# Cross-covariance attention and a multiplicative FFN on one core: scores folded into w1 and w2 per batch, norms by squares and sums, casting loads, and an order written by hand

## The chip, the core and the metric

The kernel runs on one NeuronCore of a Trainium2 chip. The metric is device microseconds for one execution, lower is better. A core has a matrix engine (PE, TensorE), a vector engine (DVE, VectorE), an engine for activation functions (ACT, ScalarE), a general one (POOL, GpSimd) and one that issues transfers (SP, SyncE). Each engine takes its instructions in the order in which they are written to it, and an instruction that waits holds all that stand behind it on the same engine. Data lies in HBM, in SBUF (128 partitions) and in PSUM (eight banks of 512 float32 numbers per partition, where matrix products are summed). A weight load (PEld in the profile) brings the stationary operand into PE; the other operand streams past, one column after another.

## The reference

There are B = 4 batches of N = 5824 tokens with C = 256 channels, and an FFN with F = 1024 inner channels. All inputs are float32.

```python
def _attn_ref(q, k, v, tau) -> np.ndarray:
    qn = q / (np.linalg.norm(q, axis=1, keepdims=True) + 1e-06)
    kn = k / (np.linalg.norm(k, axis=1, keepdims=True) + 1e-06)
    s = kn.transpose(0, 2, 1) @ qn / tau
    s = s - s.max(-1, keepdims=True)
    a = np.exp(s)
    a /= a.sum(-1, keepdims=True) + 1e-09
    return (v @ a).astype(np.float32)
...
def _moe_ref(x, w1, w2, w3, w_out) -> np.ndarray:
    a = x @ w1
    b = x @ w2
    h = a * b @ w3
    return (h @ w_out).astype(np.float32)
```

The attention is over channels, so the matrix `a` of a batch is only 256 x 256, and its norms run over all tokens of the batch. The output of the attention, `x = v @ a`, is the input of the FFN.

## The kernel before, in words

**Preparation (lines 55 to 91).** w1 and w2 are loaded as bfloat16 by casting transfers from POOL (L58, L59). w3 is cast into a scratch tensor in HBM (L70), read back transposed by eight DMA transposes (L74), and multiplied by w_out (L85), which gives one matrix W = w3 @ w_out of 1024 x 256 in bfloat16 (L91).

**Scores of a batch (lines 105 to 157).** The tokens are taken in pieces of eight tiles of 128 tokens; six pieces make 46 tiles, the last one half empty and filled with zeros (L114, L115). SP loads q, k and v as float32 (L117 to L128), each token's row of 1 KB on its own. ACT casts v and q to bfloat16 (L129, L130), DVE casts k (L131). SP transposes the bfloat16 v (L133) into `vT`, of which there is one buffer. For each tile and each half of the channels PE makes three products: the scores G (L140, 256 columns), q times q (L146, 128 columns) and k times k (L152, 128 columns). Only the diagonals of the last two are used.

**Norms and softmax of a batch (lines 159 to 194).** DVE multiplies the products by an identity matrix and sums (L163, L164, L167, L168), ACT takes roots (L165, L169), DVE inverts; a row of q norms is made with PE (L174) and spread over the partitions by POOL (L178). DVE scales the scores (L182), finds the largest (L186), ACT takes the exponential (L191), DVE divides by the sum into `a_bf` (L194).

**FFN of a batch (lines 196 to 260).** The padded tokens are taken in chunks of 512 columns, eleven and a half per batch. For each chunk PE first makes the attention's output xT, two halves of two products each (L209), which ACT copies to bfloat16 (L215). Then for each of eight blocks jt of 128 inner channels PE makes aT from w1 (L223) and bT from w2 (L229), two products of 512 columns each; ACT copies aT to `a_sb` (L236), DVE multiplies it by bT into `ab` (L238); PE multiplies `ab` by W into the output's sums (L244), four products of 256 columns. aT and bT share three PSUM banks (tag "ab"). After the eighth block ACT copies the output (L258) and SP stores it, 128 tokens at a time (L260).

**What sets the order.** A scheduler orders the instructions of each engine by priorities and puts in the waits; the loops above only tell it what depends on what. It places later batches' loads, casts and score products between FFN instructions where it finds room.

## Time and profile before

| | |
|---|---|
| runs of the kernel | 797.06, 803.74 and 807.34 us; median 803.74 us |
| span of the profiled execution | 798.2 us |
| busy in that span | PE 675.7, PEld 393.9, DVE 307.5, ACT 417.0, POOL 9.9 us |
| moved by DMA | 114.00 MB; read from HBM 78.91 MB, written 25.95 MB |
| first xT product (L209) | 118.1 us after the span's start |

The profiled execution's own time is its span, from the first to the last instruction; it lies inside the spread of the three runs and 5.5 us under their median. A busy time is the sum of what the profiler drew for an engine. For PE it says less than it seems to: matrix products are pipelined, each is drawn from its start until its result is out, so two that follow one another overlap in the drawing. How dense PE really is shows in the distance from one start to the next. "Idle before" is the time in which an engine did nothing just before an instruction, with what ended it. PEclk is the share of its full clock that PE was granted. In the DMA views, q1 is the queue of transfers issued by SP, and q0 that of transfers issued by POOL, which alone can cast; a "packet" there is one run of bytes on one of sixteen DMA engines. Bytes are those written, so a cast from float32 to bfloat16 reads twice what is shown.

### The profile page before, as it was taken

How to read it: one execution, taken by the hardware profiler on the slowest of the kernel's cores; microseconds unless marked ns; L12 is line 12 of the kernel's file. 1: busy time of each engine (PE TensorE's matmuls, PEld its weight loads, DVE VectorE, ACT ScalarE, POOL GpSimd, SP SyncE). 2: the span in 40 equal slices, each digit the busy share in tenths (PEclk: the TensorE clock that was granted, in tenths of full speed). 3: DMA queues.
4: the chain of work that ended last, by engine and by line, in shares of the span. 5: the costliest groups of instructions: out<-in, count | busy, mean ns of one | idle time of the engine just before them, and what ended most of it. 6: DMA issues, size and time to landing. Idle time of an engine off the chain costs nothing.

```text
span 798.2 us, 11457 instructions
## 1 busy us (share of the span) xinstructions
PE 675.7 (85%) x4314; PEld 393.9 (49%) x4376; DVE 307.5 (39%) x508; ACT 417.0 (52%) x761; POOL 9.9 (1%) x22
## 2 busy tenths in 40 slices
PE   3255259999998869999998869999999959999997
PEld 2134245555554565555554555555555725555554
DVE  0000044544443353444443353444444244444443
ACT  3032267755556655554556656555555345554553
POOL 2000000000000000000000000000000000000000
PEclk9578769999999989999999889999999969999999
DMA  9999999995109897411109980010119100110111
GB/s 278 215 247 298 266 329 338 290 292 189 53 27 202 274 333 230 137 64 36 53 28 216 296 260 21 33 53 27 54 38 193 39 0 27 54 54 27 53 47 44
DMA packets 155511, 114.00 MB, mean 143 GB/s; under 512 B 60672, under 2 KB 154880, under 8 KB 155392
## 3 DMA queue, kind: packets, MB, share of 16 engines
q1 hardware_dynamic: 153792, 109.60, 48.0%
q0 software_dynamic: 1664, 3.67, 2.5%
q8 instruction: 34, 0.56, 0.3%
q14 instruction: 21, 0.17, 0.1%
HBM read 78.91 MB, written 25.95 MB: 131 GB/s over the span
## 4 chain that ended last, share of the span: by engine, by line
PE 64%; DMA 13%; ACT 10%; SPq 5%; issue 5%; DVE 3%; ACTq 0%; POOLq 0%; DVEq 0%
PE out_ps L244 20%; PE bT L229 16%; PE aT L223 16%; DMA qk_f<-in_q_dram 5%; PE xT L209 5%; ACT o_sb L258 4%; SPq L133 3%; DMA v_f<-in_v_dram 3%; ACT qk_bf L130 2%; PE G_ps L140 2%; ACT a_sb L236 2%; DMA vT<-v_bf 2%; PE qk_ps L146 2%; PE qk_ps L152 2%; DMA qk_f<-in_k_dram 1%
## 5 line engine op out<-in xcount | busy, mean ns | idle before, releaser
L238 DVE TENSOR_TENSOR ab<-a_sb,bT 128x512 bf16<-128x512 bf16 (+1 forms) x384 | 255.3, 665 | 342.2 <-PE aT L223 155.3
L236 ACT CAST a_sb<-aT 128x512 bf16<-128x512 f32 (+1 forms) x384 | 215.3, 582 | 213.7 <-PE aT L223 179.3
L229 PE MATMUL bT<-xT_bf,w_sbuf 128*128 128x512 bf16 (+1 forms) x737 | 246.9, 372 | 16.1 <-ACT a_sb L236 14.0
L223 PE MATMUL aT<-xT_bf,w_sbuf 128*128 128x512 bf16 (+1 forms) x737 | 245.9, 372 | 2.0 <-ACT a_sb L236 0.3
L244 PE MATMUL out_ps<-W_sbuf,ab 128*128 128x256 bf16 x1472 | 226.7, 275 | 4.0 <-DVE ab L238 0.7
L244 PEld LDWEIGHTS <-ab 128*128 128x128 bf16 x1472 | 123.1, 98 | 124.7 <-DVE ab L238 89.5
L140 PE MATMUL G_ps<-qk_bf 128*128 128x256 bf16 x368 | 88.3, 294 | 36.3 <-DVE qk_bf L131 25.5
L146 PE MATMUL qk_ps<-qk_bf 128*128 128x128 bf16 x368 | 83.3, 244 | 30.9 <-ACT qk_bf L130 29.4
L229 PEld LDWEIGHTS <-w_sbuf 128*128 128x128 bf16 x768 | 75.3, 98 | 66.1 <-issue 20.8
L223 PEld LDWEIGHTS <-w_sbuf 128*128 128x128 bf16 x768 | 75.5, 98 | 62.0 <-issue 7.4
L152 PE MATMUL qk_ps<-qk_bf 128*128 128x128 bf16 x368 | 83.5, 244 | 0.1
L129 ACT CAST v_bf<-v_f 128x2048 bf16<-128x2048 f32 (+1 forms) x24 | 43.9, 1830 | 62.0 <-DMA v_f<-in_v_dram 56.4
L209 PE MATMUL xT<-vT,a_bf 128*128 128x512 bf16 (+1 forms) x192 | 67.1, 377 | 6.3 <-DVE r_inv L184 3.9
L131 DVE CAST qk_bf<-qk_f 128x2048 bf16<-128x2048 f32 (+1 forms) x24 | 28.3, 1179 | 108.3 <-DMA qk_f<-in_k_dram 98.7
L215 ACT CAST xT_bf<-xT 128x512 bf16<-128x512 f32 (+1 forms) x96 | 55.2, 575 | 19.1 <-PE xT L209 17.8
L258 ACT COPY o_sb<-out_ps 128x256 f32<-128x256 f32 (+1 forms) x184 | 55.5, 391 | 13.8 <-PE out_ps L244 13.5
L130 ACT CAST qk_bf<-qk_f 128x2048 bf16<-128x2048 f32 (+1 forms) x24 | 43.9, 1831 | 31.3 <-DMA qk_f<-in_q_dram 22.4
L140 PEld LDWEIGHTS <-qk_bf 128*128 128x128 bf16 x368 | 38.6, 105 | 43.6 <-DVE qk_bf L131 37.0
L146 PEld LDWEIGHTS <-qk_bf 128*128 128x128 bf16 x368 | 41.0, 112 | 35.3 <-ACT qk_bf L130 30.1
L152 PEld LDWEIGHTS <-qk_bf 128*128 128x128 bf16 x368 | 40.9, 111 | 12.0 <-issue 2.6
L209 PEld LDWEIGHTS <-a_bf 128*128 128x128 bf16 x192 | 18.7, 98 | 30.2 <-issue 4.4
L174 PE MATMUL qn_row_ps<-identity_f,qn_col 128*1 128x128 f32 x8 | 2.3, 395 | 20.7 <-DVE tmp L167 20.7
(37 smaller groups left out, 79.5 us busy)
## 6 DMA issues: line engine op xcount, KB each, us to landing
out_dram<-o_sb SPq DMA_DIRECT2D x180, 128.0 KB, 1.8
qk_f<-in_q_dram SPq DMA_DIRECT2D x20, 1024.0 KB, 7.8
qk_f<-in_k_dram SPq DMA_DIRECT2D x20, 1024.0 KB, 10.4
v_f<-in_v_dram SPq DMA_DIRECT2D x20, 1024.0 KB, 8.5
qk_f<-in_q_dram SPq DMA_DIRECT2D x4, 640.0 KB, 8.5
qk_f<-in_k_dram SPq DMA_DIRECT2D x4, 640.0 KB, 9.1
v_f<-in_v_dram SPq DMA_DIRECT2D x4, 640.0 KB, 8.5
scratch_w_bf<-in_moe_w_dram POOLq DMA_DIRECT2D x1, 2048.0 KB, 17.6
```

The lines of the kernel that those rows point to most:

```text
L130: nc.scalar.copy(qk_bf[:, :nt, :C], qk_f[:, :nt, :C])
L140: nc.tensor.matmul(G_ps[:, ct, :], lhsT=qk_bf[:, i, C + ct * P:C + (ct + 1) * P], rhs=qk_bf[:, i, :C], start=first, stop=last,)
L146: nc.tensor.matmul(qq_ps[:, ct, :], lhsT=qk_bf[:, i, ct * P:(ct + 1) * P], rhs=qk_bf[:, i, ct * P:(ct + 1) * P], start=first, stop=False,)
L152: nc.tensor.matmul(kk_ps[:, ct, :], lhsT=qk_bf[:, i, C + ct * P:C + (ct + 1) * P], rhs=qk_bf[:, i, C + ct * P:C + (ct + 1) * P], start=Fal ...
L209: nc.tensor.matmul(xT_ps[:, :ncur], lhsT=a_bf[:, c1t, c2t * P:(c2t + 1) * P], rhs=vT[:, n0 // P:(n0 + ncur) // P, c1t, :], start=(c1t == 0 ...
L215: nc.scalar.copy(xT_bf[:, c2t, :ncur], xT_ps[:, :ncur])
L223: nc.tensor.matmul(aT_ps[:, :ncur], lhsT=w1_sbuf[:, ct, jt * P:(jt + 1) * P], rhs=xT_bf[:, ct, :ncur], start=(ct == 0), stop=(ct == CT - 1),)
L229: nc.tensor.matmul(bT_ps[:, :ncur], lhsT=w2_sbuf[:, ct, jt * P:(jt + 1) * P], rhs=xT_bf[:, ct, :ncur], start=(ct == 0), stop=(ct == CT - 1),)
L236: nc.scalar.copy(a_sb[:, :ncur], aT_ps[:, :ncur])
L238: nc.vector.tensor_mul(ab[:, :ncur], a_sb[:, :ncur], bT_ps[:, :ncur])
L244: nc.tensor.matmul(out_ps[:, ns, :], lhsT=ab[:, ns * P:(ns + 1) * P], rhs=W_sbuf[:, jt, :], start=(jt == 0 and z_start), stop=(jt == FT - ...
L258: nc.scalar.copy(o_sb[:nvalid, ns, :], out_ps[:nvalid, ns, :])
```

## The change

The program is written anew; what it computes for each output is the same up to rounding, with the softmax's subtraction of the maximum left out.

- **Token order.** Of each batch, the first 45 x 128 tokens are loaded as `(p i) c -> p i c`: partition p holds tokens 45p to 45p+44, so that a piece of eight tiles is 8 KB in one run per partition. The 64 tokens that are left form a short last tile. The output is stored in the same order, four rows or 4 KB per partition (L318).
- **Loads.** q, k, v, w1, w2, w3 and w_out are all loaded by POOL with a cast to bfloat16 on the way (L101, L102, L339, L340, L352, L353). The casts on ACT and DVE are gone. SP has only transposes and stores.
- **Norms.** The products q times q and k times k are gone. ACT squares q and k, two tiles at a time (L146), DVE adds the squares up in float32 (L158, L171), PE sums over partitions with a column of ones (L179), and ACT makes the root with Ln and Exp (L184, L185). The k norms are spread along a row by PE (L195).
- **Scores folded into the weights.** The product is now q times k (L149), so that after the exponential `e` can be the stationary operand. Instead of xT = a^T vT for each chunk, the kernel makes a @ w1 and a @ w2 once for each batch (`Wf`: L232 on PE, then L238 on ACT and L240 on DVE, which also divide by the sums), and the FFN takes vT itself as its streaming operand (L282). The stage xT and its copies are gone.
- **FFN.** Chunks are 512 columns, eleven per batch, and a twelfth of 192. aT and bT share four PSUM banks, the output has three of 512 numbers. ACT and DVE copy one half of the output each (L316, L317), and one store of 512 KB per chunk takes it away.
- **Order.** The scheduler is off (`manual_schedule`); each engine's order is that of the calls. A table of calls with due times (`make_agenda`) is run down between FFN blocks as a counter of estimated PE time goes on. The output products follow their block two blocks later (LAG). In the first batch they are put off until W is made (L370), at 31 units of the counter and later, and up to 46 blocks of `ab` wait in SBUF. Batch 0's scores run ahead of all FFN work.

Two buffers of `vT` let the next batch's v be transposed while this one's is used.

```diff
+    ctx.enter_context(tc.manual_schedule())
+
+    nc.scalar.preload_act_table_set("natural_log_exp_and_others")
...
+    def load_piece(nm, n, pi):
+        pool = v_pool if nm == "v" else qk_pool
+        t = pool.tile([P, PIECE, C], BF16, tag=nm, name=f"{nm}_{n}_{pi}")
+        main, left = qk_main[nm, n]
+        g = LAST if pi == NP_ - 1 else PIECE
...
+        nc.gpsimd.dma_start(out=t[:, :g, :], in_=main[:, pi * PIECE : pi * PIECE + g, :])
+        pieces[nm, n, pi] = t
...
+                nc.scalar.activation(out=dst[:, :, part, :], in_=src[:, o : o + 2, :], func=AF.Square)
+                i = o + part
+                for ct in range(CT):
+                    nc.tensor.matmul(
+                        G[:, ct, :],
+                        lhsT=qt[:, i, ct * P : (ct + 1) * P],
+                        rhs=kt[:, i, :],
...
+            elif pr > 0:
+                nc.vector.tensor_add(accs[n], accs[n], sqs[0])
...
+        def fold(i):
+            h, rest = divmod(i, 4)
+            w, c1 = divmod(rest, 2)
+            m = psum.tile([P, 512], F32, tag="ab", name=f"fold_{n}_{i}", bufs=4)
+            for c2 in range(CT):
+                nc.tensor.matmul(
+                    m, lhsT=st["e"][:, c2, c1 * P : (c1 + 1) * P], rhs=w12[:, c2, w, h * 512 : (h + 1) * 512],
+                    start=(c2 == 0), stop=(c2 == CT - 1),
+                )
+            dst = Wf[n][:, c1, w, h * 512 : (h + 1) * 512]
+            if i % 2 == 0:
+                nc.scalar.activation(out=dst, in_=m, func=AF.Copy, scale=st["rs"][:, c1 : c1 + 1])
+            else:
+                nc.vector.tensor_scalar_mul(dst, m, st["rs"][:, c1 : c1 + 1])
...
+    def emit_ab(b, c, j):
+        n = chunk_cols(c)
+        tiles = []
+        for w in range(2):
+            t = psum.tile([P, 512], F32, tag="ab", name=f"{'ab'[w]}_{b}_{c}_{j}", bufs=4)
+            for ct in range(CT):
+                nc.tensor.matmul(
+                    t[:, :n], lhsT=Wf[b][:, ct, w, j * P : (j + 1) * P], rhs=rhs_of(b, c, ct),
+                    start=(ct == 0), stop=(ct == CT - 1),
+                )
+            tiles.append(t)
...
+        nc.scalar.copy(a_sb[:, :n], tiles[0][:, :n])
...
+        nc.vector.tensor_mul(ab[:, :n], a_sb[:, :n], tiles[1][:, :n])
+        pend.append((b, c, j, ab))
...
+            for jt in range(FT):
+                at(31.0 + jt, 0.87, lambda jt=jt: w_unit(jt))
...
     for b in range(B):
...
-                        nc.tensor.matmul(
-                            qq_ps[:, ct, :],
...
-                        nc.tensor.matmul(
-                            kk_ps[:, ct, :],
...
-                xT_bf = work_pool.tile([P, CT, NCHUNK], DT.bfloat16, tag="xT")
...
+        make_agenda(b)
+        for c in range(NCH):
+            for j in range(FT):
+                run_due()
+                emit_ab(b, c, j)
+                npop = 0
+                while w_ready[0] and len(pend) > LAG and npop < 2:
+                    emit_out(*pend.pop(0))
+                    npop += 1
+                    run_due()
+        run_due(1e9)
```

**Where instructions now stand.** The first place is PE in the middle of the FFN. Before, in the last batch (each product has a weight load ahead of it, mostly left out here; aT_7689 and bT_7690 are the block that follows aT_7675 and bT_7676):

```order
L223 MATMUL aT_7675<-xT_bf,w_sbuf 128x512
...
L244 MATMUL out_ps<-W_sbuf,ab 128x256
...
L229 MATMUL bT_7676<-xT_bf,w_sbuf 128x512
...
L223 MATMUL aT_7689<-xT_bf,w_sbuf 128x512
...
L244 MATMUL out_ps<-W_sbuf,ab 128x256
...
L229 MATMUL bT_7690<-xT_bf,w_sbuf 128x512
```

The change, in batch 1 and chunk 8 (a_8_4 and b_8_4 are block 4's two products, abs_8_1 and abs_8_2 the operands of blocks 1 and 2, o_8 the output's sums, q_5 and k_5 a piece of batch 2):

```order
L303 MATMUL o_8_1_3359<-W_sb,abs_8_1_3335 128x256
L149 LDWEIGHTS q_5_2859
L149 MATMUL G_2285<-k_5_2863,q_5_2859 128x256
...
L282 MATMUL a_8_4_3383<-vT_939,Wf_1913 128x512
...
L282 MATMUL b_8_4_3386<-vT_939,Wf_1913 128x512
L303 LDWEIGHTS abs_8_2_3356
L303 MATMUL o_8_0_3358<-W_sb,abs_8_2_3356 128x256
```

Before, a block's aT stood ahead of the output products and its bT behind them, and the next block's aT followed at once. Now a block's four products stand together, then the output products of the block two earlier, and score products of the next batch come between.

The second place is the start of the program. Before, SP's queue of loads began so:

```order
L117 DMA qk_f<-in_q_dram 128x8x256
L118 DMA qk_f<-in_k_dram 128x8x256
L119 DMA v_f<-in_v_dram 128x8x256
L117 DMA qk_f<-in_q_dram 128x8x256
L118 DMA qk_f<-in_k_dram 128x8x256
L133 DMA_TRANSPOSE vT<-v_bf 128x16x128
L119 DMA v_f<-in_v_dram 128x8x256
```

Of POOL's queue in the change, these are some of the rows up to its sixteenth load, in their order (row by row q_0 to q_5 and k_0 to k_5 are the pieces of batch 0, w and w_bf are w1 with w2, and w3):

```order
L102 DMA k_1_93<-in_k_dram 128x2048
masks.py:197 MEMSET ident 128x128
masks.py:199 ISA
masks.py:199 AFFINE_SELECT ident<-ident 128x128
L102 DMA q_2_99<-in_q_dram 128x2048
...
L102 DMA v_0_175<-in_v_dram 128x2048
...
L102 DMA k_5_213<-in_k_dram 128x1280
L339 DMA w_83<-in_moe_w_dram 128x2x1024
...
L102 DMA v_1_219<-in_v_dram 128x2048
L102 DMA v_2_221<-in_v_dram 128x2048
L352 DMA w_bf<-in_moe_w_dram 128x8x1024
L353 DMA wout_sb<-in_moe_w_out_dram 128x8x256
```

Loads of q, k and v came from SP in turn, with a transpose between them; now all come from POOL, q and k of the whole batch ahead of most of v and of the weights, and an instruction that makes an identity matrix stands among them.

The third place is SP in the change, with the transposes of batch 0's v, of w3 and of batch 1's v, and the first stores:

```order
L116 DMA_TRANSPOSE vT_311<-v_0_175 128x16x128
L116 DMA_TRANSPOSE vT_311<-v_1_219 128x16x128
L116 DMA_TRANSPOSE vT_311<-v_2_221 128x16x128
L359 DMA_TRANSPOSE w3T_315<-w_bf 128x32x128
L359 DMA_TRANSPOSE w3T_316<-w_bf 128x32x128
L116 DMA_TRANSPOSE vT_311<-v_3_385 128x16x128
...
L116 DMA_TRANSPOSE vT_939<-v_0_865 128x16x128
L318 DMA out_dram<-osb_0_994 128x1024
L318 DMA out_dram<-osb_1_1094 128x1024
L116 DMA_TRANSPOSE vT_939<-v_1_1017 128x16x128
```

w3's two transposes stand behind three pieces of v, and each later transpose stands ahead of stores that queue behind it.

473 lines of the change are left out of this document (288 added, 185 removed).

## The prediction, on record before the result

> **What bounds the kernel now.** I read the page's busy times first, then the chain that ended last, then a table by stretches.
>
> ```profile
> span 798.2 us, 11457 instructions
> PE 675.7 (85%) x4314; PEld 393.9 (49%) x4376; DVE 307.5 (39%) x508; ACT 417.0 (52%) x761; POOL 9.9 (1%) x22
> PE 64%; DMA 13%; ACT 10%; SPq 5%; issue 5%; DVE 3%; ACTq 0%; POOLq 0%; DVEq 0%
> 0.00:118.00 118.00, 46.67 (x376) 37.97 (x377) 13.50 (x29) 34.76 (x32) 5.74 (x13) 0.75 1.06 271
> 300.00:420.00 120.00, 118.73 (x692) 63.96 (x704) 52.19 (x75) 66.68 (x137) 0.00 (x0) 1.00 0.29 90
> 640.00:650.00 10.00, 2.72 (x6) 0.68 (x8) 4.67 (x19) 3.66 (x8) 0.55 (x1) 0.51 0.00 0
> ```
>
> The last three rows are stretches: length, then busy time of PE, PEld, DVE, ACT and POOL, then the granted clock, the DMA share and GB/s. For 118 us the DMA engines are full and PE is mostly idle; then PE is the bound, but for a hole at 640. How dense is PE in its own stage? The timeline tells, by starts:
>
> ```profile
> 739.81 1.21 ACT L258 COPY o_sb<-out_ps 128x256 f32<-128x256 f32 x4
> 740.00 0.38 PE L223 MATMUL aT<-xT_bf,w_sbuf 128*128 128x512 bf16 x1
> 740.21 0.38 PE L229 MATMUL bT<-xT_bf,w_sbuf 128*128 128x512 bf16 x1
> 740.43 0.59 PE L223 MATMUL aT<-xT_bf,w_sbuf 128*128 128x512 bf16 x2
> 752.29 1.21 ACT L258 COPY o_sb<-out_ps 128x256 f32<-128x256 f32 x4
> 280.28 0.22 PE L146 MATMUL qk_ps<-qk_bf 128*128 128x128 bf16 x1
> 280.33 0.22 PE L152 MATMUL qk_ps<-qk_bf 128*128 128x128 bf16 x1
> 280.39 0.27 PE L140 MATMUL G_ps<-qk_bf 128*128 128x256 bf16 x1
> 280.50 0.22 PE L146 MATMUL qk_ps<-qk_bf 128*128 128x128 bf16 x1
> ```
>
> A product of 512 columns holds PE for 0.215 us, one of 256 for 0.109, one of 128 for 0.055. A chunk has 36 of the first (4 of them xT) and 32 of the second, 11.25 us, but the output copies of two chunks are 12.48 us apart: PE loses 1.23 us per chunk to its neighbours.
>
> **What goes, on PE.** xT, 4 x 0.215 = 0.86 us per chunk in 46 chunks (11.5 per batch), 40 us. The products q times q and k times k, 184 x 0.055 = 10 us per batch. The padding: 11.5 chunks become 11 and a short one.
>
> **What PE then has to do once the FFN has begun.** A chunk is 32 x 0.215 + 32 x 0.109 = 10.38 us; 44 of them make 456.7. A short chunk (192 columns, 0.083 us each by interpolation) is 32 x 0.083 + 16 x 0.109 = 4.4; four make 17.6. W: 64 x 0.109 = 7.0. Scores of three batches: 3 x 92 x 0.109 = 30.1. Folds of three batches: 3 x 16 x 0.215 = 10.3. Small products: about 3. Sum **525 us**, at the granted clock of 1.00 that the dense stretch shows.
>
> **Does PE stay the bound?** The groups with shapes kept apart:
>
> ```profile
> L238 DVE TENSOR_TENSOR ab<-a_sb,bT 128x512 bf16<-128x512 bf16 x352 | 242.0, 688 | 323.5 <-PE aT L223 155.3 <-ACT a_sb L236 136.1 <-PE bT L229 24.9
> L236 ACT CAST a_sb<-aT 128x512 bf16<-128x512 f32 x352 | 203.7, 600 | 202.3 <-PE aT L223 169.8 <-remote 16.9 <-DVE ab L238 9.2
> L130 ACT CAST qk_bf<-qk_f 128x2048 bf16<-128x2048 f32 x20 | 38.0, 1902 | 21.9 <-DMA qk_f<-in_q_dram 12.9 <-PE qk_ps L152 4.7 <-PE G_ps L140 4.1
> L130 ACT CAST qk_bf<-qk_f 128x1536 bf16<-128x1536 f32 x4 | 5.9, 1474 | 9.5 <-DMA qk_f<-in_q_dram 9.5
> L182 DVE TENSOR_TENSOR s_f<-G_ps,qn_row 128x256 f32<-128x256 f32 x8 | 3.3, 415 | 2.9 <-POOL qn_row L178 2.9
> L163 DVE TENSOR_TENSOR tmp<-qk_ps,identity_f 128x128 f32<-128x128 f32 x8 | 2.3, 292 | 17.3 <-PE qk_ps L152 17.2
> ```
>
> The trace has no square of 512 columns; the casts give 0.84 ns per column and 0.19 us, so 0.62 us, between ACT's own copy of 0.60 and half the cast of 1.90. It has no float32 sum of 1024 columns; L182 and L163 give 0.96 ns per column, so 1.15 us, with 0.69 (as the product of 512) and 2.3 (twice) as bounds. ACT then has per batch 88 x 0.60 + 46 x 0.62 + 15 us (short chunk, output copies, folds, softmax, priced as L236) = 96 us, and DVE 88 x 0.69 + 22 x 1.15 + 16 = 102, at the upper bound 127. PE has 131 in such a batch (4.4 and 11 x 10.38 for the FFN, 10.0 and 3.4 for scores and folds), so both stay under it. Block by block: a block holds PE for 4 x 0.215 + 4 x 0.109 = 1.30 us, its product is ready about 2 us after its start (aT 0.64, copy 0.60, product 0.69), and its bank is wanted two blocks later, at 2.6 + 0.43 us. A square or a sum ahead of it fits into that. Before W is there, blocks come every 0.86 us and the spare is 0.2 us. So I cost the queues at 10 us in all, with 0 and 54 (44 chunks x 1.23) as the ends; if this cover failed, the banks of bT would be late first.
>
> **The start.** A cast transfer's price stands in the DMA view of two windows, 19 to 36 us and 24 to 30 us; the transposes' in 596 to 613 us:
>
> ```profile
> q0 software_dynamic: 1068, 2.92, 90.1%
> q1 hardware_dynamic: 1064, 0.68, 21.8%
> q0 software_dynamic: 48, 1.57, 121.5%
> q1 hardware_dynamic: 48, 0.05, 3.0%
> q1 hardware_dynamic: 10656, 3.07, 98.1%
> vT<-v_bf SPq DMA_TRANSPOSE x6, 4.6
> 1.27 1.02 POOL L58 DMA_DIRECT2D w_sbuf<-in_moe_w_dram  x1 [0.33 <-issue]
> 13.22 0.57 POOL masks.py:199 TENSOR_SCALAR_AFFINE_SELECT identity_f<-identity_f 128x128 f32<-128x128 f32 x1 [10.93 <-issue]
> 17.34 17.61 SPq L133 DMA_TRANSPOSE vT<-v_bf  x1
> ```
>
> 2.92 MB in 0.901 x 17 us is 191 GB/s written. A piece of 0.52 MB takes 2.75 us, q and k of a batch (5.96 MB) 31, v half of that. POOL's instruction at 13.22 stood idle for 10.93 us first. Now it stands behind four loads (11 us of transfers, issued from 1.3 us on in up to 1.02 us each, as the row of L58 shows) and ahead of the rest, which are issued at about 4.5 + 10.9 + 1 = 16.5 us, while the first four end near 13.5: a hole of 4 us, between 0 and 5. So v's first piece lands at 2.5 + 30 + 4 + 1 = 38 us, and k's last at 43.
>
> The Trainium skill, in GPSIMD Engine Reference, Instruction dispatch, gives about 6 us for the first call into freshly loaded code. The row shows 10.93 us, and by the page's 6 the hole would be gone and the sum 4 us less.
>
> From k's last piece to the FFN stands a chain. In the trace it is these two rows, 10 us from one to the other:
>
> ```profile
> 637.74 0.30 DVE tmp L163
> 647.80 0.62 PE xT L209
> ```
>
> The new chain has no products with an identity and no maximum, but three squares, the sums, Ln, Exp, two more products on PE and four folds: I take 15, between 10 and 18. So by the chain the FFN begins at 58.
>
> **A queue that the transposes now meet.** In both windows q0 and q1 moved as many packets, 1068 and 1064, 48 and 48: an engine takes one from each queue in turn, whatever their size, and the transpose begun at 17.34 held SP for 17.61 us. Six transposes and four stores (128 runs each) are 10656 packets, so a piece of v is about 1690, or 106 per engine. Behind v's first piece stand, per engine, 24 runs of q and k, 32 of w1 and w2, 16 of v, 64 of w3. One for one, the transpose ends when 3.8 MB (the first 106 of these, in part of w3) are through: 20 us, and 2.4 of its own. So 38 + 23 = **61 us** for the FFN's begin, 58 if they don't meet, 75 if the next transposes are late too. By the same count v's second and third pieces are through at about 75 and 86, and w3's two transposes, among the next loads of q and k, near 108 and 113, while PE wants W at 61 + 31 = 92. That would be 15 us of waiting, or none if they don't meet; I take 8.
>
> The Trainium skill says in DMA: Bandwidth & Descriptors, Queues, rings and completion order, that an engine changes rows only at the end of a packet of typically 9 to 17 descriptors. The rows show turns of one by one. By the page a transpose would need a dozen turns, and the sum would be that of the second rival.
>
> **In the later batches** the same queues carry 8.9 MB of loads (47 us), six transposes (14) and 6 MB of stores (22 at the first stretch's 271 GB/s), in 131 us; q and k buffers come free one by one as scores are made, so loads come in small groups and a transpose meets 16 runs, 5 us. A chunk has two output buffers, 10 us of patience. I cost them at nothing; uncovered it would be a few us per batch.
>
> **The end.** The last output product starts at 793.83 before, and the span ends at 798.2: 4 us, and I keep 4.
>
> ```profile
> 793.83 0.39 PE L244 MATMUL out_ps<-W_sbuf,ab 128*128 128x256 bf16 x2 [0.45 <-DVE ab L238]
> ```
>
> **Sum:** 61 + 525 + 8 + 10 + 4 = 608 us against the profiled span of 798.2. The runs' median lies 5.5 us above that span, their lowest 1.1 below; I add 2 and forecast **610 us**.
>
> **Rivals.**
> - *The queues still cost PE what they cost now.* For it: DVE's 0.69 of 0.86 us before W, and waits of DVE on ACT and PE all along its row. Against it: four banks for three, and two blocks between product and use. 54 us in place of 10: 654.
> - *Transposes and loads don't meet as counted* (turns of many packets). FFN from 58, no wait for W: 608 - 11 + 2 = 599.
> - *Casting loads at half the rate.* Nothing in the rows says so for runs of 4 KB; w_out's runs of 512 bytes are among those that made the 191 GB/s. Start 31 us later, and 125 of 131 us in each batch: about 650.
> - *Slower than before: SP is held by its transposes.* Place: eight transposes per later batch, each ahead of stores. If each held SP as the one at 17.34 did, 17.6 us, 10 of them covered by the output buffers, that is 24 x 7.6 = 182: 790. From a hold of 19 us on (24 x 8.8 more than 608) it is over 820, slower. Against it: one for one, a batch's transposes can't wait for more runs than there are, 47 us of them.
> - *ACT or DVE becomes the bound* only beyond 131 us per batch, over the upper bound above; no time given.
>
> **Chances.** Forecast 0.70; second rival 0.10; first 0.10; third 0.07; fourth 0.03. The likeliest one's own range is 590 to 635: begin 58 to 75, wait for W 0 to 15, queues 0 to 20, not all at one end. The two slow ones reach 654; the range is **585 to 655**. Only the fourth leaves the faster side by 2%, which is about what a measurement of this kernel can tell from no change: faster 0.97, same 0.01, slower 0.02.
>
> **What would show it.** First L282 product near 61 us; the last batch's output copies 10.4 us apart; PE idle before L370 for about 8 us, ended by a DMA; L158 near 1.15 and L146 near 0.62 us; granted clock 1.00 from 65 us on. It is wrong if chunks of the last batch take over 11 us, if L146 waits for loads after the first batch, or if stores stand behind transposes while PE waits for output banks.

## The result, and the profile after

| | before | after |
|---|---|---|
| median of the runs shown with the result | 803.63 us | 616.50 us (606.25 to 619.94) |
| ratio, with its 95% interval | | 0.760 (0.752 to 0.768) |
| span of the profiled execution | 798.2 us | 612.9 us |
| first FFN product (before: first xT) | 118.1 us | 59.0 us |
| output copies, from one chunk of the last batch to the next | 12.48 us | 10.40 us |

The forecast was 610 us, with 585 to 655 as its range: the time lies inside, and so does its sign. Ratios are taken from undisturbed runs alone, so that they need not be the quotient of the medians given. The first views of the changed kernel, by page and by stretches (length, busy time of PE, PEld, DVE, ACT and POOL with counts, granted clock, DMA share, GB/s):

```profile
span 612.9 us, 9631 instructions
PE 561.3 (92%) x3564; PEld 353.0 (58%) x3568; DVE 396.9 (65%) x566; ACT 360.6 (59%) x657; POOL 51.2 (8%) x102
```

```profile
0.00:59.00 59.00, 25.90 (x123) 16.43 (x124) 32.17 (x35) 32.12 (x56) 13.68 (x29) 0.82 1.05 196
92.00:103.00 11.00, 7.57 (x52) 4.94 (x51) 4.49 (x8) 3.44 (x7) 0.00 (x0) 0.96 1.13 222
103.00:167.00 64.00, 64.00 (x459) 45.40 (x458) 44.45 (x56) 42.23 (x78) 9.66 (x19) 0.98 1.08 186
167.00:190.00 23.00, 15.10 (x92) 9.76 (x91) 9.82 (x13) 7.85 (x15) 2.41 (x5) 0.78 1.10 175
190.00:609.00 419.00, 415.71 (x2705) 262.08 (x2706) 282.75 (x423) 254.64 (x468) 19.03 (x38) 1.00 0.42 98
```

From 190 us on PE is busy for 415.7 of 419 us at full clock: the FFN of the later batches is as dense as forecast. What PE loses, it loses in three places of the first batch: the start, a wait near 100, and a hole between 167 and 190 that the prediction did not have. Three timelines of the changed kernel show what ended each. First PE (in brackets the idle time and what ended it):

```profile
59.03 1.03 PE L282 MATMUL a<-vT,Wf 128*128 128x512 bf16 x2 [6.97 <-DMA vT<-v]
182.48 0.58 PE L303 MATMUL o<-W_sb,abs 128*128 128x256 bf16 x2 [7.90 <-ACT osb L316]
```

then ACT's copies of the output, one per chunk:

```profile
157.02 0.58 ACT L316 COPY osb<-o 128x512 f32<-128x512 f32 x1 [0.19 <-PE o L303]
165.06 0.58 ACT L316 COPY osb<-o 128x512 f32<-128x512 f32 x1 [0.19 <-PE o L303]
181.84 0.58 ACT L316 COPY osb<-o 128x512 f32<-128x512 f32 x1 [9.25 <-DMA out_dram<-osb]
191.42 0.58 ACT L316 COPY osb<-o 128x512 f32<-128x512 f32 x1 [0.45 <-PE o L303]
```

then SP's queue, where the duration is the time for which the instruction held SP (called its hold; x2 is two holds in a row):

```profile
30.89 1.44 SPq L116 DMA_TRANSPOSE vT<-v  x1
43.41 15.86 SPq L116 DMA_TRANSPOSE vT<-v  x1
72.75 27.57 SPq L359 DMA_TRANSPOSE w3T<-w_bf  x2
151.21 17.36 SPq L116 DMA_TRANSPOSE vT<-v  x1
168.67 1.83 SPq L318 DMA_DIRECT2D out_dram<-osb  x2
170.59 16.14 SPq L116 DMA_TRANSPOSE vT<-v  x1
```

Last, two rows of the DMA view, of the transpose issued at 151.21 and of the first store issued at 168.67; the last number is the time from issue to landing:

```profile
vT<-v SPq DMA_TRANSPOSE x1, 28.4
out_dram<-osb SPq DMA_DIRECT2D x1, 512.0 KB, 13.1
```

Read backwards: PE waited at 174 for ACT's copy, and ACT from 172.6 on for a buffer whose store landed at 181.8. That store held the copy of 157.02. It stood on SP behind a transpose until 168.67, and then took 13.1 us to land, where the median store of this profile takes 3.3; the transpose ahead of it landed at 179.6, 2 us before it. So the store was late by the whole time of that transpose, 28.4 us to its landing, and not by the hold of 17.4 alone. A chunk of output came every 8.0 us then (157.02, 165.06), because the backlog of blocks is worked off at two per block. With two buffers a store then has some 15 us from the copy until its buffer is wanted again; this one took 24.

The two groups that the prediction priced without a row of their own, and the wait for W:

```profile
L158 DVE TENSOR_TENSOR acc<-acc,sq 128x1024 f32<-128x1024 f32 x88 | 107.3, 1220 | 11.7 <-ACT sq L146 9.5
L146 ACT ACTIVATE sq<-q 128x512 f32<-128x512 bf16 x88 | 55.6, 632 | 3.6 <-DVE acc L158 3.3
L369 PE MATMUL w<-wout_sb,w3T 128*128 128x256 bf16 x64 | 9.3, 305 | 3.4 <-DMA w3T<-w_bf 3.4
```

### The profile page after: what moved, and what is told of

Its sections match the earlier page's. It is cut to its first block, busy times and chain, and to the rows that moved or that the text cites. A ratio compares the mean times of both kernels' runs of the same rounds, so it can differ in the third digit from the quotient of the medians.

```text
span 612.9 us, 9631 instructions
## 1 busy us (share of the span) xinstructions
PE 561.3 (92%) x3564; PEld 353.0 (58%) x3568; DVE 396.9 (65%) x566; ACT 360.6 (59%) x657; POOL 51.2 (8%) x102
## 3 DMA queue, kind: packets, MB, share of 16 engines
q0 software_dynamic: 13952, 39.46, 36.1%
## 4 chain that ended last, share of the span: by engine, by line
PE 78%; DMA 12%; SPq 6%; DVE 1%; ACT 1%; issue 1%; POOL 0%; POOLq 0%; ACTq 0%
PE o L303 25%; PE a L282 22%; PE b L282 22%; PE G L149 5%; SPq L116 5%; DMA w3T<-w_bf 4%; DMA k<-in_k_dram 4%; DMA v<-in_v_dram 2%; DMA out_dram<-osb 2%; PE fold L232 2%; SPq L359 1%; PE w L369 1%; ACT as L288 1%; DVE abs L290 1%; PE ss L179 1%
## 5 line engine op out<-in xcount | busy, mean ns | idle before, releaser
L290 DVE TENSOR_TENSOR abs<-as,b 128x512 bf16<-128x512 bf16 (+1 forms) x384 | 252.0, 658 | 169.8 <-ACT as L288 134.4
L288 ACT CAST as<-a 128x512 bf16<-128x512 f32 (+1 forms) x384 | 215.7, 562 | 187.2 <-PE a L282 96.4
L303 PE MATMUL o<-W_sb,abs 128*128 128x256 bf16 x1472 | 222.5, 274 | 8.1 <-ACT osb L316 7.9
L282 PE MATMUL a<-vT,Wf 128*128 128x512 bf16 x704 | 211.4, 382 | 7.1 <-DMA vT<-v 7.0
L282 PEld LDWEIGHTS <-Wf 128*128 128x128 bf16 x1536 | 150.1, 99 | 111.5 <-DMA vT<-v 7.5
L282 PE MATMUL b<-vT,Wf 128*128 128x512 bf16 x704 | 211.3, 382 | 0.0
L303 PEld LDWEIGHTS <-abs 128*128 128x128 bf16 x1472 | 143.9, 98 | 91.9 <-issue 8.6
L158 DVE TENSOR_TENSOR acc<-acc,sq 128x1024 f32<-128x1024 f32 x88 | 107.3, 1220 | 11.7 <-ACT sq L146 9.5
L149 PE MATMUL G<-k,q 128*128 128x256 bf16 x368 | 69.5, 297 | 20.1 <-DMA k<-in_k_dram 20.1
L146 ACT ACTIVATE sq<-q 128x512 f32<-128x512 bf16 x88 | 55.6, 632 | 3.6 <-DVE acc L158 3.3
L149 PEld LDWEIGHTS <-q 128*128 128x128 bf16 x368 | 39.0, 106 | 28.2 <-issue 11.3
L146 ACT ACTIVATE sq<-k 128x512 f32<-128x512 bf16 x88 | 55.2, 627 | 0.0
L317 DVE COPY osb<-o 128x512 f32<-128x512 f32 x44 | 30.1, 685 | 8.3 <-DMA out_dram<-osb 7.4
L316 ACT COPY osb<-o 128x512 f32<-128x512 f32 x44 | 25.8, 586 | 13.9 <-DMA out_dram<-osb 9.2
L102 POOL DMA_DIRECT2D q<-in_q_dram x24 | 13.3, 553 | 198.0 <-ACT sq L146 162.8
L102 POOL DMA_DIRECT2D v<-in_v_dram x24 | 13.1, 551 | 62.4 <-DMA vT<-v 55.9
L232 PE MATMUL fold<-w,e 128*128 128x512 bf16 x60 | 17.5, 423 | 0.8 <-ACT as L288 0.5
L238 ACT ACTIVATE Wf<-fold,rs 128x512 bf16<-128x512 f32 x16 | 11.0, 687 | 11.7 <-PE fold L232 7.4
L240 DVE TENSOR_SCALAR Wf<-fold,rs 128x512 bf16<-128x512 f32 x16 | 11.8, 748 | 5.2 <-PE fold L232 5.1
L102 POOL DMA_DIRECT2D k<-in_k_dram x24 | 13.4, 558 | 1.6 <-DMA q<-in_q_dram 1.3
L232 PEld LDWEIGHTS <-e 128*128 128x128 bf16 x64 | 6.8, 107 | 7.4 <-issue 3.9
## 6 DMA issues: line engine op xcount, KB each, us to landing
v<-in_v_dram POOLq DMA_DIRECT2D x20, 512.0 KB, 11.6
```

What stands on the lines that cost most here:

```text
L102: nc.gpsimd.dma_start(out=t[:, :g, :], in_=main[:, pi * PIECE : pi * PIECE + g, :])
L146: nc.scalar.activation(out=dst[:, :, part, :], in_=src[:, o : o + 2, :], func=AF.Square)
L149: nc.tensor.matmul(G[:, ct, :], lhsT=qt[:, i, ct * P : (ct + 1) * P], rhs=kt[:, i, :], start=(pr == 0 and part == 0 and ct == 0), stop=(pr ...
L158: nc.vector.tensor_add(accs[n], accs[n], sqs[0])
L232: nc.tensor.matmul(m, lhsT=st["e"][:, c2, c1 * P : (c1 + 1) * P], rhs=w12[:, c2, w, h * 512 : (h + 1) * 512], start=(c2 == 0), stop=(c2 == ...
L282: nc.tensor.matmul(t[:, :n], lhsT=Wf[b][:, ct, w, j * P : (j + 1) * P], rhs=rhs_of(b, c, ct), start=(ct == 0), stop=(ct == CT - 1),)
```

## The experiments

Each kernel is the change with one edit, unless it says otherwise. Times are medians of the kernel's runs; 801 to 804 us is the kernel before beside them. The change itself spans 606 to 634 us in its ten runs, and most kernels have one profile, so a gain or loss of a few us in a median says little; what is read is each profile's waits.

**The change once more.** It had six more runs and a second profile.

> The change once more, unaltered, so that it has as many runs as the variants and a second profile. If the hold of SP by a transpose depends on which loads it happens to meet, the holds before 210 us differ from the first profile by several us each, the chunks after 210 us don't (10.4 us in the last batch, 11.5 in the others), and the runs spread over 600 to 625 us, with the difference between two profiles made wholly before 210 us. If the spread has another cause (the clock, the stores), the later batches differ too.

628.4 us, 607.8 to 633.8; ratio 0.763 (0.757 to 0.770). The profiled span was 606.0. There the output copies of the same stretch are evenly spaced:

```profile
160.38 0.58 ACT L316 COPY osb<-o 128x512 f32<-128x512 f32 x1 [0.19 <-PE o L303]
168.42 0.58 ACT L316 COPY osb<-o 128x512 f32<-128x512 f32 x1 [0.19 <-PE o L303]
176.46 0.59 ACT L316 COPY osb<-o 128x512 f32<-128x512 f32 x1 [0.50 <-PE o L303]
184.28 0.58 ACT L316 COPY osb<-o 128x512 f32<-128x512 f32 x1 [0.45 <-PE o L303]
```

The longest hold of SP between 110 and 210 us was 10.4 us instead of 17.4, there is no hole, and from 212 us on the chunks of both profiles are equal to 0.1 us. The first profile's two long chunks (16.8 and 9.6 us for 8.0 each) cost 10.4 us; the second had a longer wait for W (5.8 us for 3.4) and was 3.4 us later from there on: that leaves the 7 us between them. The transpose that landed 28.4 us after its issue in the first profile landed after 19.6 here, and the store behind it 1.2 us before the copy that took its buffer again. So the hole comes and goes from run to run with the transposes' time to landing. That the wider spread of the other runs is the same thing was not seen, since they have no profile.

**Transposes against loads, at the start.** w3 and w_out are loaded behind v's fourth piece, which waits for v's first transpose.

```diff
-    nc.gpsimd.dma_start(out=w3_bf, ...)      # ahead of the folds
-    nc.gpsimd.dma_start(out=wout_sb, ...)
             at(0.0, 0.0, lambda: load_piece("v", 0, 3))
+            at(0.0, 0.0, load_w3)
```

> The loads of w3 and w_out are issued behind the fourth piece of v, which waits until v's first piece is transposed; all else is as in the change. Theory 1 (the transposes of v's first pieces share the DMA engines run for run with the casting loads behind which they were issued): without 2.5 MB of loads beside it the first transpose is through near 46 instead of 59 us, the FFN begins when the folds are done, near 52, and w3T is done at about the same time as before or a few us earlier; the span is near 606. Theory 2 (the transpose takes its 28 us whatever the loads do, or waits for v's second piece): FFN still begins at 59, w3T later, span 613 to 620. If W comes later than the FFN's earlier start allows, half the gain goes into a longer wait before L369 (3.4 us now).

616.7 us (605.8 to 628.1), ratio 0.758 (0.753 to 0.763), span 604.4. PE's timeline:

```profile
46.53 5.27 PE L232 MATMUL fold<-w,e 128*128 128x512 bf16 x16
51.63 0.59 PE L282 MATMUL a<-vT,Wf 128*128 128x512 bf16 x2
```

The FFN follows the folds without a wait, 7.4 us earlier, as theory 1 has it: the transpose was late only for the loads beside it. But w3T was ready at 101.7, hardly earlier than before (102.5), and PE, earlier by then, waited 14.0 us for it instead of 3.4. The whole gain went into the next transfer. (The lower span is that of a profile without the late hole.)

**The wait for W.** Three pairs of loads for the second batch are moved from 16, 20 and 30 units to 34, 38 and 42.

```diff
-                at(16.0, 0.0, lambda: load_qk(1, 1))
+                at(34.0, 0.0, lambda: load_qk(1, 1))
```

> The loads of the second batch's q and k pieces 2 to 4 are due at 34, 38 and 42 units instead of 16, 20 and 30, so that they don't run beside the transposes of w3; all else is as in the change. Theory 1 (w3's transposes share the DMA engines run for run with those loads): w3T is through by about 88 us instead of 102.5, PE doesn't wait before L369 (3.4 us now, 3.5 to 5 us with the slow clock behind it), and the span up to 110 us gains 4 us. The loads meet v's transposes later, so the hole at 174 us may grow or shrink; by itself the span is about 608. Theory 2 (the transposes take their 30 us alone): w3T still ends near 102 and nothing is gained.

623.0 us (599.7 to 636.7), span 614.8. SP was free of w3's transposes at 92.5 instead of 100.3, and W's products began at 91.6 and waited for nothing: the wait is explained, though w3T was ready at 94.6, later than the 88 of theory 1. The loads then met v's transposes; PE waited 12.5 us for an output copy, and no time was gained in the median. What that copy waited for was a store issued at 117.96, ahead of the next hold (21.4 us at 120.6); it landed at 139.5, 3 us after the transpose ahead of it, which was issued at 106.85 and landed at 136.3.

**Stores on another engine.** The stores are issued by ACT.

```diff
-                nc.sync.dma_start(out=rows[:, 4 * c : 4 * c + 4, :], in_=o)
+                nc.scalar.dma_start(out=rows[:, 4 * c : 4 * c + 4, :], in_=o)
```

> The stores of whole chunks (L318) are issued by ACT instead of SP, so that no store stands behind a transpose; all else is as in the change. Theory 1 (a store waits behind a transpose that holds SP for 17 us, and while 46 blocks of backlog are worked off at two per block a chunk's output is complete every 6 us, so two output buffers cover only some 6 us): PE has no hole near 174 us, L316 waits for no store, and the span is about 10 us shorter, near 603. ACT waits for DVE's half of each output copy, under 1 us per chunk, which its spare time hides. Theory 2 (the store itself is slow because the DMA engines are full of casting loads): the wait of L316 for out_dram stays, and the span is within 3 us of 613. Theory 3 (ACT is delayed by the wait before each store, 44 times about 1 us): the hole goes but later chunks are longer than 10.4 us and the span is 613 or more.

645.2 us, span 631.8: none of the three theories. (Five runs took 614.3 to 649.6; a sixth took 1028.8 us at a granted clock of 0.66, which nothing here explains. The lowest lies inside the change's own spread, so the loss is not in every run.) ACT's timeline, then SP's:

```profile
153.86 0.59 ACT L316 COPY osb<-o 128x512 f32<-128x512 f32 x1 [2.78 <-DMA out_dram<-osb]
172.63 0.36 ACTq L318 DMA_DIRECT2D out_dram<-osb  x1
173.04 0.63 ACT L146 ACTIVATE sq<-q 128x512 f32<-128x512 bf16 x1 [18.59 <-DMA vT<-v]
```

```profile
114.49 62.09 SPq L116 DMA_TRANSPOSE vT<-v  x5
```

ACT stood 18.6 us before a store, and what ended it was a transpose. In this program's list of waits the transfers of SP and ACT take eight completion semaphores in turn, and a new transfer waits for the one that had its semaphore before. For the store at 172.63 that one was the transpose issued at 142.26, which landed only at 172.53. (SP's row merges five transposes with the waits between them; the longest single hold was 12.7 us.) The dependence had only moved to an engine that PE waits for sooner (16.5 us at L282).

**A third output buffer.** Four of 46 buffers of ab pay for it.

```diff
-            o = work.tile([P, 4, D], F32, tag="o_sb", ..., bufs=2)
+            o = work.tile([P, 4, D], F32, tag="o_sb", ..., bufs=3)
```

> Three buffers of the output copies (osb) instead of two, and 42 buffers of ab instead of 46 to make room; all else, SP's order included, is as in the change. Theory 1 (stores stand behind transposes that hold SP for 16 to 17 us, and in the backlog a chunk of output comes every 8 us): a third buffer gives 8 us more patience, so of the hole of 8 us in PE near 174 us (10 us with the low granted clock behind it) at most 2 are left and the span is 603 to 606. Theory 2 (the DMA engines themselves are behind, and any number of buffers fills up): the hole only moves to a later chunk, span 610 or more. If the first theory holds, the spread between runs shrinks too, since the hold differs from run to run.

613.6 us (605.0 to 629.5), ratio 0.757 (0.753 to 0.762), span 605.7. With holds of 14.6 and 12.1 us all chunks of the backlog are 8.0 us apart. That is no proof of the third buffer: the change's second profile has no hole with two. By the landings here (160.7 and 199.4, where the copies that would have wanted those two buffers stood at 160.5 and 196.4) it saved 0.2 and 3.1 us. The spread did not shrink, so that part of the expectation failed, and the gain in the median is within the spread.

**Short runs.** q and k of all batches in plain token order, 1 KB read and 512 bytes written per run; each score is the same sum, its tokens taken in another order.

```diff
+            order = "(p i) c -> p i c" if nm == "v" else "(i p) c -> p i c"
-                src[n, : NT * P, :].rearrange("(p i) c -> p i c", i=NT),
+                src[n, : NT * P, :].rearrange(order, i=NT),
```

> q and k alone are loaded in the plain token order, each token's row a run of 1 KB read and 512 bytes written, eight times as many runs as in the change (the scores sum over tokens, so the order is free); v and the output stay partition-contiguous. Theory 1 (queues take turns run by run, whatever the size): a transpose that meets q and k loads now waits for runs an eighth as long, so the holds of SP at 151 and 171 us shrink from 17 us to under 8, the hole in PE at 174 goes, and if the casting rate stays near 200 GB/s the span is near 603. Theory 2 (short casting runs are slower, say half the rate): k's last piece of the first batch lands near 60 instead of 33 us, the FFN begins at 80 or later and the span is 635 or more. Theory 3 (neither): within 3 us of 613.

623.7 us, 622.3 to 628.5; ratio 0.780 (0.776 to 0.784); span 621.9. Both theories hold in part. From 120 to 200 us a transpose held SP for 5.1 to 7.2 us, never 16. But loading cost more: in the DMA rows of the whole span, casting loads (q0) of the change and then of this kernel,

```profile
q0 software_dynamic: 13952, 39.46, 36.1%
```

```profile
q0 software_dynamic: 53888, 39.46, 45.7%
```

took 221 us of the sixteen engines in the change (36.1% of 612.9) and 284 here. FFN began at 62.5, w3's transposes held SP until 108, and the span is 9 us over the change's first. And a hole of 4.7 us was left near 170, where SP was not held: there two stores took 20.5 and 12.9 us to land, the first of them 1 us after the transpose issued ahead of it at 147.34, which had held SP for only 6.0 us but landed after 26.4. So the partition-contiguous order of q and k is worth having for the loads and costs something at the transposes. The runs are steady, within 6 us.

**The order of PE's products.** A block's a, then the previous block's output products, then its b.

```diff
         for w in range(2):
+            if w == 1 and mid and pend:
+                emit_out(*pend.pop(0))
```

> The order of PE's products is that of the kernel before: a block's a, then the output products of the block before it, then its b (in place of a, b, then the output products of the block two earlier); four banks as in the change. Theory 1 (the two blocks between product and use are what removed the 1.23 us per chunk): DVE's product begins when b ends and takes 0.69 us, the cover is the next a's 0.43 us, so PE waits in each block, and the last batch's chunks take 11.6 us or more (12 by 0.2 us a block); the span is 660 to 690. Theory 2 (the loss before came from the xT stage and its copies, not from the order): chunks of the last batch stay at 10.4 us and the span is 613 to 625.

773.6 us (773.4 to 774.2), ratio 0.966 (0.961 to 0.971). Theory 1 has the direction, at more than twice its size. The last batch's chunks are 15.5 us apart, 1.94 us per block. The groups say why:

```profile
L305 PE MATMUL o<-W_sb,abs 128*128 128x256 bf16 x1472 | 227.5, 275 | 117.6 <-DVE abs L292 117.4
L284 PE MATMUL b<-vT,Wf 128*128 128x512 bf16 x704 | 211.1, 382 | 0.0
```

PE waits for DVE's product ahead of every group of output products, and DVE's 0.69 us begin only when b is done. So the distance between a block and its output products is worth some 157 us. I had taken the 1.23 us per chunk of the kernel before as the price of this very order. But its order is another, as its PE shows in the last batch:

```profile
748.56 0.60 PE L244 MATMUL out_ps<-W_sbuf,ab 128*128 128x256 bf16 x4
748.99 0.38 PE L229 MATMUL bT<-xT_bf,w_sbuf 128*128 128x512 bf16 x1
749.21 0.60 PE L244 MATMUL out_ps<-W_sbuf,ab 128*128 128x256 bf16 x4
749.64 0.38 PE L223 MATMUL aT<-xT_bf,w_sbuf 128*128 128x512 bf16 x1
749.86 0.38 PE L229 MATMUL bT<-xT_bf,w_sbuf 128*128 128x512 bf16 x1
750.08 0.59 PE L223 MATMUL aT<-xT_bf,w_sbuf 128*128 128x512 bf16 x2
750.70 0.59 PE L229 MATMUL bT<-xT_bf,w_sbuf 128*128 128x512 bf16 x2
751.61 0.60 PE L244 MATMUL out_ps<-W_sbuf,ab 128*128 128x256 bf16 x4
```

It takes the output products of two blocks close together (748.56 and 749.21), then six products of the next two blocks and here two of xT (left out), and only then output products again. So this run prices half a block of distance, not the order of the kernel before; what its 1.23 us per chunk were spent on stays open.

**Three banks and one block of distance.** In place of four and two.

```diff
-LAG = 2
+LAG = 1
-            t = psum.tile([P, 512], F32, tag="ab", ..., bufs=4)   # and the five others of this tag
+            t = psum.tile([P, 512], F32, tag="ab", ..., bufs=3)
```

> Three PSUM banks for aT and bT instead of four and the output products one block behind instead of two, as the kernel before had it within half a block; all else is as in the change. Theory 1 (the fourth bank and the second block are what removed the 1.23 us per chunk that PE lost to its neighbours): with the squares and sums between, a chunk takes 11 to 11.6 us, 30 to 54 us more, 640 to 667. Theory 2 (a block's bank and product come in time anyway in a block of 1.30 us; the loss before came from the scheduler's order and the copies of xT): last batch's chunks stay at 10.4 us, scoring batches lose at most 0.3 us at each tile pair, 14 us per batch at the very most, and the span is 615 to 635.

637.1 us (621.3 to 642.9), span 641.0. The last batch's chunks stay at 10.40, those of the scoring batches go from 11.5 to about 11.8, 5 us per batch: theory 2 by its mechanism, though the span lies outside its 615 to 635. The other 15 us of the longer span arose before 231 us, with a wait of PE for an output copy of 14.0 us near 149. So the first whole block of distance is what counts; the second, with the fourth bank (the two were not tried apart), is worth some 11 us over the batches after the first (5 in each scoring batch and 1 in the last).

**The identity on POOL.** A partition_broadcast is added behind all work.

```diff
+    nc.gpsimd.partition_broadcast(spread, row1[:1, 0])
```

> One partition_broadcast on POOL, the instruction that the kernel before used at L178 and the change does without, is added behind all work, on data that nothing reads. Theory 1 (the 10.93 us that POOL stood idle ahead of the identity in the kernel before were the loading of code that this program needs for partition_broadcast): POOL stands idle for some 11 us at the identity again, q's and k's third pieces are issued near 16 us, first scores and FFN begin some 4 us later, and the span is 617 to 625. Theory 2 (the idle time had to do with the transfers issued ahead of it, or with the DMA engines being busy): no idle time at the identity, and the span is that of the change plus a few us at the end.

630.7 us (one run), span 628.9. POOL's row of the identity in the change, then in this kernel:

```profile
3.79 0.29 POOL masks.py:199 TENSOR_SCALAR_AFFINE_SELECT ident<-ident 128x128 f32<-128x128 f32 x1
```

```profile
15.46 0.28 POOL masks.py:199 TENSOR_SCALAR_AFFINE_SELECT ident<-ident 128x128 f32<-128x128 f32 x1 [11.54 <-issue]
```

An instruction at the very end brings back 11.5 us at the start, and FFN begins at 63.9, 4.9 us later. Theory 1 holds: the idle time belongs to a program that uses partition_broadcast, not to the identity. The rest of the longer span is mostly a late hole, with a hold of 22.0 us at 173.1 and 13.1 us of waiting on PE.

**Three repairs together:** w3 late, q and k late, three output buffers.

> Three edits together: loads of w3 and w_out behind v's fourth piece, the second batch's q and k pieces 2 to 4 later, three output buffers (42 of ab). If each stall has the cause that I gave it, FFN begins near 47 to 52 us, w3T is through near 88, PE waits for W at most 3 us, and no hole stands at 174: 52 + 530 of products + 6 of small losses + 4 = 592 to 597. If a stall only moves on to the next transfer, 603 or more.

607.6 us (605.5 to 618.2), ratio 0.759 (0.754 to 0.764), span 604.4. FFN begins behind the folds and the wait for W is 3.7 us, close to the 3 expected; the hole is not gone, and the span is that of the expectation's second sentence, 603 or more. PE waited 7.9 us for an output copy at 139.9. The store it needed was issued at 115.08, ahead of the hold of 23.9 us at 119.4, and took 24.8 us to land; the transpose ahead of it, issued at 103.33, took 33.7.

**The same with runs a quarter as long** for q and k of the later batches, 2 KB read and 1 KB written (again the scores' tokens are only taken in another order).

```diff
-        nc.gpsimd.dma_start(out=t[:, :g, :], in_=main[:, pi * PIECE : pi * PIECE + g, :])
+            nc.gpsimd.dma_start(
+                out=t[:, :g, :].rearrange("p (h i) c -> p h i c", i=i),
+                in_=src[n, ...].rearrange("(h p i) c -> p h i c", p=P, i=i),
+            )
```

> The three edits of the last combination (w3 and w_out behind v's fourth piece, second batch's q and k later, three output buffers), and q and k of the later batches loaded in runs of 2 KB read and 1 KB written in place of 8 and 4 KB. Theory (a hold of SP is the number of transpose packets per engine, about 106, times the time of the load run that each takes its turn with): with runs a quarter as long the holds before 210 us stay under 14 us, where the last combination had 23.9 and 28.2; three buffers cover that, no hole stands in PE between 100 and 200 us, and the span is 594 to 598. Rival (holds go by the bytes that are under way, however they are cut): a hold of over 20 us stays and with it a hole of some 8 us, 603 to 610. Second rival (shorter runs load more slowly): L146 waits for loads in the first or a later batch, 605 or more.

**598.55 us, 597.6 to 602.5; ratio 0.748 (0.745 to 0.752)**: the best of all, and its seven runs lie within 4.9 us. (The profile is that of the slowest of them.) SP's queue in the last kernel and in this one:

```profile
103.33 11.66 SPq L116 DMA_TRANSPOSE vT<-v  x1
119.38 23.89 SPq L116 DMA_TRANSPOSE vT<-v  x1
```

```profile
103.63 12.44 SPq L124 DMA_TRANSPOSE vT<-v  x1
122.31 11.63 SPq L124 DMA_TRANSPOSE vT<-v  x1
```

The second transpose, with the same pieces of load issued around it, holds SP half as long and lands after 21.2 us for 38.5. One later hold is 16.6, over the 14 expected; PE has no hole between 103 and 190. The second rival's sign, a wait of the squares for loads, is not there after the start. But W was waited for 6.1 us, and early in the second batch PE waited 3.9 us for an output copy, again behind transposes that landed late (its store landed at 218.9, the last transpose ahead of it at 213.7). In a stretch where both queues have work they moved as many packets each, now of a quarter the size (122 to 128 us of this kernel):

```profile
q0 software_dynamic: 881, 0.93, 90.1%
q1 hardware_dynamic: 880, 0.34, 32.4%
```

**Those runs alone,** without the three repairs.

> Of the last combination only the shorter load runs are kept: q and k of the later batches in runs of 2 KB read and 1 KB written; w3's place, the due times and the two output buffers are those of the change. Theory (the spread and the late holes come from turns with 4 KB runs): FFN still begins at 59 and W is still waited for (3 to 7 us), but no transpose holds SP for 17 us before 210 us, the hole in PE between 160 and 190 is under 4 us, the runs lie within 6 us of each other as those with 512-byte runs did (the change's lie 28 us apart), and the median is 604 to 610. Rival (two buffers are too few for any hold over 8 us, so short runs alone don't help): holes of 4 us and more stay in several chunks, 612 or more. Second rival (it was the three output buffers and the later loads that made the last combination steady): the runs spread over more than 15 us.

612.8 us (610.2 to 622.8), ratio 0.768 (0.762 to 0.773), span 610.2. No hold between 118 and 210 us was over 10.7 and the backlog's chunks are all 8.0 us apart, which speaks against the first rival. But the change's second profile, with long runs, has the same (10.4), so one profile does not show that the short runs did it. The wait for W rose to 11.1 us, 7.7 more than in the change's first profile, and by that the median missed its range. Five of the six runs lie within 5.4 us, the sixth 7 above them: 12.6 us in all, between the theory's 6 and the second rival's 15, so that of the steadiness it remains open how much each of the edits gives.

## Why the prediction was right, and where it was not

Time by time, the profiled span against the sum:

| term | predicted | measured |
|---|---|---|
| FFN begins | 61 | 59.0 |
| PE's products from there on | 525 | 527 (counted by groups, at the same durations) |
| wait for W | 8 | 3.4 |
| hole in the late first batch | 0 | 10 (23.0 us of stretch, 12.5 of products in it) |
| waits of PE for ACT and DVE ("the queues") | 10 | 3 |
| PE's lower clock and the rest | 0 | 6, of them 3 by a granted clock of 0.80 in the first 14 us |
| end | 4 | 4 |

The sum came out 5 us low, and that is closer than its terms: the hole and the lower clock, both put at nothing, and the products took 19 us more than forecast, and the begin, the wait for W and the queues 14 less. That much of the hit is luck.

- **The bound.** Right: PE is dense, ACT and DVE stay under it. The last batch's chunks are 10.40 us for 10.38; squares 0.63 for 0.62, sums 1.22 for 1.15. The first rival (54 us lost to the queues) falls with the 10.40. (PE's 131 us for a later batch add up to 132 by their own terms, and it took 135; nothing hangs on that.) The granted clock was 1.00 in the 419 us from 190 on, but not from 65 on as forecast: 0.78 in the stretch with the hole.
- **The start.** Right in sum, with errors that cancel, which is luck. "A hole of 4 us, between 0 and 5": there is none, and the loads ran at 214 GB/s for 191, so v's first piece landed at 30.9 instead of 38 and k's last at 34.4 instead of 43; the chain behind it took 17.7 us for 15. The step that failed is that the 10.93 us belonged to the instruction; the broadcast experiment shows what they belong to. The Trainium skill's 6 us (GPSIMD Engine Reference, Instruction dispatch) for freshly loaded code fits neither: 10.93 and 11.54 with the broadcast, nothing without it. And the transpose took 28.1 us for 23. That it met the loads is shown by moving them away (16.6 us).
- **The wait for W.** Its place and cause are right (shown by the late loads), its size smaller: w3T's halves were done at 81.5 and 102.5, not 108 and 113, and PE came to the second half only at 99.1, not at 92.
- **The step that failed** is the term at nothing: "a transpose meets 16 runs, 5 us. A chunk has two output buffers, 10 us of patience. I cost them at nothing". For the later batches, for which it was worked out, it holds: transposes held SP for 1 to 10 us and landed within 13, and PE did not wait. The late first batch had no term of its own. There the prediction's own sign of being wrong came true, stores behind transposes while PE waits for output banks: it is the fourth rival's mechanism, at one place instead of 24, 10 us in the first profile and nothing in the second. Its numbers do not fit there. The backlog brings a chunk every 8.0 us, where I had used the 10.4 of a later batch; even so two buffers give a store some 15 us, more than the 10. What was missed is that a store waits until the transpose ahead of it has landed, which takes longer than its hold. In all six kernels with a hole before 215 us the store that PE waited for landed 1 to 4 us after the transpose issued ahead of it, also where it had hardly stood on SP (short runs):

| kernel | transpose issued, us to landing | store issued, us to landing | ACT's copy | PE waited |
|---|---|---|---|---|
| the change | 151.21, 28.4 | 168.67, 13.1 | 181.84 | 7.9 |
| short runs | 147.34, 26.4 | 154.28, 20.5 | 174.91 | 4.7 |
| q and k late | 106.85, 29.4 | 117.96, 21.5 | 139.54 | 12.5 |
| three banks | 115.27, 29.2 | 124.71, 23.6 | 148.37 | 14.0 |
| three repairs | 103.33, 33.7 | 115.08, 24.8 | 139.92 | 7.9 |
| broadcast at the end | 173.10, 36.3 | 195.24, 18.0 | 213.28 | 13.1 |

In none of the twelve profiles with stores on SP's queue did a store land before the transpose issued ahead of it. That the order of the queue makes it so is argued: the one run that took the stores off SP's queue made them wait for transposes by semaphores. (In the last row PE waited through ACT's copies for the next batch's weights, which stood behind the output copy.)

- **Turn by turn.** The packets' counts (881 and 880) and the shorter holds in two kernels (5 to 7 us with runs of 512 bytes, 11.6 for 23.9 with 1 KB) bear out the one-for-one count; the 10.7 us of the short runs alone say nothing, since the change's second profile has 10.4. The Trainium skill (DMA: Bandwidth & Descriptors, Queues, rings and completion order) gives packets of typically 9 to 17 descriptors for one turn. Equal counts over many turns can't tell such turns from turns of one; the prediction's 48 to 48 packets in 6 us, three of each queue per engine, leave little room for them. Yet the count doesn't give the longest times. Beside the change's hold of 16.1 us at 170.59 only two pieces were issued, 16 runs per engine, which by the count are 5 us. The DMA view of 12 to 30 us in the change, with loads alone, and of the first 5 us of the 23.9 us hold in the three repairs' kernel (119 to 124):

```profile
q0 software_dynamic: 1051, 3.85, 106.4%
```

```profile
q0 software_dynamic: 42, 0.16, 67.9%
q1 hardware_dynamic: 205, 0.05, 67.0%
```

A load run took 0.29 us of an engine in the first (106.4% of 288 engine-us by 1051) and 1.3 us in the second (67.9% of 80 by 42), and there the queues moved 42 to 205 packets, one to five. What slowed both queues there stays open.

Of the 185 us between the spans, 59 come from the earlier begin. 40 are xT and 30 the products q times q and k times k of three batches, both by the prediction's prices; some 3 are padding. Against these stand 10 for the folds of three batches and 7 for W, which is now made behind the FFN's begin. The other 70 or so are what PE lost in the stages before and loses no more; which part of the change took how much of them away was not tried.

## What to carry to other kernels

Where one queue issues both transposes that must wait and stores that others wait for, count a store as late until the transpose ahead of it has landed (28.4 us where SP was held for 17.4), and the patience of the output buffers at the fastest rate at which output is made, not at the mean. Moving one transfer away only passed the wait on while the DMA engines were full; what helped was to move the loads, to cut the other queue's runs shorter and to add a buffer, all together. Keep at least one whole block of products between what PE makes and what it needs back.

## What the runs showed of the hardware

- A partition_broadcast at the end of POOL's program cost 11.5 us at its start, ahead of an instruction that without it ran at once.
- A store issued on SP behind a transpose landed after it in all twelve profiles, so a transpose delays the stores behind it even when it no longer holds SP (6.0 us held, 26.4 to landing, in the kernel with short runs).
- Runs of 512 bytes written made the casting loads 28% dearer in engine time than the change's mix of mostly 4 KB (284 for 221 us). Runs of 1 KB for the later batches cost less: 40.4% of 600.7, 243 us.
- After a wait PE ran at a lower granted clock: 0.78 in the stretch with the late hole, and 0.80 in the first 14 us of the FFN, where PE was never idle, with 1.00 in the 419 us from 190 us on. The row of those 14 us:

```profile
59.00:73.00 14.00, 13.97 (x52) 5.80 (x53) 8.04 (x12) 7.25 (x13) 2.16 (x4) 0.80 1.14 208
```
